# Six instead of three first-layer products per unit by the inner scheme, with the operations ordered by a table

## Chip, cores and metric

The kernel runs on one core of a Trainium2 chip. The metric is the device time of one launch in microseconds; less is better. All data are float32.

## The reference

```python
# q, k, v: (8 batches, 8 heads, 576 tokens, 64);  w_in (512, 2048);  w_out (2048, 512);  alpha (2048)
k_p = k.reshape(B, H, 72, 8, D).mean(axis=3)
v_p = v.reshape(B, H, 72, 8, D).mean(axis=3)
scores = np.matmul(q, k_p.transpose(0, 1, 3, 2)) / np.sqrt(D)
attn = np.exp(scores - scores.max(axis=-1, keepdims=True))
attn = attn / (attn.sum(axis=-1, keepdims=True) + 1e-09)
x = np.matmul(attn, v_p).transpose(0, 2, 1, 3).reshape(4608, 512)
h = x @ w_in
s = np.sin(alpha * h)
g = h + s * s / (alpha + 1e-09)
out = g @ w_out
```

So it is an attention over pooled keys and values, and behind it two matrix products with a sine nonlinearity between them.

## The kernel before, in words

**Stages.** There are eight batches of 576 tokens for the attention and nine units of 512 tokens for the first layer. While unit u runs through the first layer, the attention of batch u+1 is computed beside it, so that its values are there when unit u+1 starts. The results g of the first layer go to a buffer in DRAM (`g_bridge`). The second layer (`outputs`, line 1312 for its matmuls) then runs over the eight batches and reads g back.

**Products.** Both layers use a scheme of Strassen's kind: a product of 2 x 2 blocks is computed with seven products of blocks instead of eight. In the first layer a unit has four column groups J = 0 to 3, and each has seven products, numbered 1 to 7: 28 products in a unit. A plain product (`product`, line 834) is four matmuls of 128 x 128 weights with 256 columns. It adds into a PSUM bank; `begin` takes the four banks b1, b6, b5 and b7 of a group from five that rotate (0 to 4). Banks 5 to 7 serve the attention and the intermediate results of the inner scheme.

**Inner scheme.** `inner_product` (line 1014) computes a product once more by seven smaller ones, each one matmul with 128 columns. It comes in four pieces: `a` (two matmuls into bank 6 or 7, then two ACT copies, lines 1018 and 1020), `b` (two matmuls, one ACT copy, line 1024), `d` (one matmul, one DVE add, line 1029) and `e` (two matmuls). Each piece needs the copies of the one before, so other matmuls are written between the pieces. In units 1 to 6 it is used for product 5 of J = 2 and 3 and for product 1 of J = 3: three products of 28. The sums that it needs are made by GpSimd (POOL): those of the weights once, in unit 0 (`inner_w_in`), those of x in each unit (`inner_x`).

**Around a product.** ACT copies b1 to b6, b6 to b7 and b5 to the tile p5 (line 810), computes the sines (984) and squares (991). DVE adds p5 and the sines (809) and finishes a group (`finish`, 1036), then SP stores its g (`store_g`, 1050). The tile for g has two buffers, so group J+2 writes where group J was stored from.

**The attention's steps.** For one batch: `k_t` (keys transposed), `two_scores` (scores, in two blocks of 64 and 80 recorded matmuls, line 308), shifts (the row maximum is taken and subtracted, DVE, 331 and 332), `exp` on ACT (357), `norm` (row sums on DVE, product on POOL, 365), `turn` (DVE transposes, 491 to 501), `move` (16 transfers, 511), `all_values` (600 and 613, and ACT copies into x, 527). `turn_q` transposes a later batch's q on DVE (219, 224) and moves it with 16 transfers (234). `load_k`, `load_v` and `load_q` fetch, and POOL adds the rows that are pooled (131). `sums_of_x` forms the four sums of x that the products take (DVE, 804).

**Order.** The program is written out by hand: `hidden` runs over 28 slots of a unit, seven to a column group, and `carry` says which attention step goes into which slot. Each engine executes its instructions in the order in which the program issues them, and SP's queue holds back all transfers behind one that waits. In the kernel before, the two blocks of scores are in slots 3 and 5 (in front of products 2 and 3 - that is, behind products 6 and 7 - of J = 0), the exps in slots 8 to 10, the values in slot 25.

Of the kernel before, what the change touches and what calls it, by code (L numbers as in the profile page):

```python
# [24 lines left out]

class Kernel:
    def __init__(self, tc, q, k, v, w_in, w_out, alpha, out):
        self.tc, self.nc = tc, tc.nc
# [12 lines left out]
        self.T = self.S // 4  # L56

        self.gd = self.nc.dram_tensor("g_bridge", (2, self.NJ * JW, P, self.B * self.S), F32, kind="Internal").ap()

    def home(self, i, shape):  # L60

        return (self.xp if i < 2 else self.xq).tile(shape, F32, name=f"home{i}")
# [15 lines left out]
    def q_tile(self, i):  # L78

        return self.qp.tile([P, 5 * self.H * self.D], F32, name=f"q{int(i)}")  # L80
# [35 lines left out]
    def load_k(self, b, e):  # L116
# [3 lines left out]
        t = self.kvp.tile([P, 2048], F32, name="kvin")[:NP * m, 0:3 * POOL * D]  # L120
        self.nc.sync.dma_start(out=t, in_=self.k[b, NP * e:NP * e + NP].rearrange("h (p x) d -> (h p) (x d)", x=3 * POOL))
        if b not in self.kp:
            self.kp[b] = self.ap.tile([NP * m, 3, 2, D], F32, name="kp")
# [9 lines left out]
    def load_v(self, b):  # L133

        nc, D, H = self.nc, self.D, self.H
        vm, vz = self.vp[b] = self.ap.tile([P, H // 2, D], F32, name="vm", bufs=2), self.ap.tile([P, H // 2, D], F32, name="vz", bufs=2)
        t = self.kvp.tile([P, 2048], F32, name="kvin")[:].rearrange("p (h x) -> p h x", h=4)
        x = self.kvp.tile([P, POOL * D], F32, name="vr", bufs=1)[:]
# [40 lines left out]
    def load_v_rows(self, b, main, rest):  # L179
# [6 lines left out]
        self.vp[b] = self.ap.tile([P, self.H // 2, self.D], F32, name="vm", bufs=2), self.ap.tile([P, self.H // 2, self.D], F32, name="vz", bufs=2)  # L186
# [19 lines left out]
    def turn_q(self, b, part):  # L206
# [8 lines left out]
        if part == 0:  # L215
            for e in range(2):
# [3 lines left out]
                if e == 0:  # L220
                    self.finish_before()
# [17 lines left out]
    def new_tr(self):  # L239
        return self.ap.tile([P, 20 * 5 * 32], F32, name="tr")[:]  # L240
# [8 lines left out]
    def attention(self, b):  # L249
# [44 lines left out]
        def two_scores(j):  # L294

            x = (self.turn + 1) % 5
# [22 lines left out]
        def shifts(i, m, ps):  # L319
# [6 lines left out]
            for z, o in zip(ps, y):  # L326
                w = list(z.shape)[:-1]
                mx = self.sm.tile([P, 12], F32, name="mx2")[:, 0:m * (1 + i % 2)]
# [15 lines left out]
        def shift(i, e, ps):  # L344

            n = rows[i]
            mx = self.sm.tile([P, NP], F32, name="mx")
# [11 lines left out]
        def norm(i):  # L359

            n = E(i).shape[1]
            sm = self.sm.tile([P, 12], F32, name="sm2")[:, 0:n]
# [4 lines left out]
        def new_a():  # L367
            self.aM = self.ap.tile([P, 4, 736], F32, name="aM")
# [71 lines left out]
        def norm_rest():  # L440

            n = 64
            sm = self.sm.tile([P, H], F32, name="sm")
# [146 lines left out]
        def all_values():  # L590
# [16 lines left out]
            nc.scalar.copy(out=self.sm.tile([P, 1], F32, name="order")[:], in_=rest[:, 1, 0:1])  # L607
# [7 lines left out]
            self.behind_order()  # L615
            self.behind_order = lambda: None
# [152 lines left out]
    def inner_w_in(self):  # L769

        w = self.q_tile(0)[:]
        at = 0
        for p, J0 in ((5, 2), (1, 3)):
            n = self.NJ - J0
# [31 lines left out]
    def hidden(self, u, extra):  # L806
# [7 lines left out]
        def begin(J):  # L814
# [5 lines left out]
            if two and J > 1:  # L820
                G.i5 = self.inner_product(G, 5, b5, 7)
# [757 lines left out]
```

## Time and profile before

| quantity | value |
|---|---|
| timed runs | 906.38, 906.35, 905.76 us; median 906.35 us |
| profiled execution | span 902.6 us from its first to its last instruction; no time of its own is given beside it |
| what lies around the span | 906.35 - 902.6 = 3.75 us by the median |
| start of unit 1 (k transpose in front of it) | 84.44 us |
| units 1 to 6, period | 55.06 us |
| last product of the first layer ends | about 515 us |
| second layer, PE without a stop | 537.40 to 898.3 us |
| 16 DMA engines, busy share in a middle unit | 0.68 to 0.71 |
| granted TensorE clock | 1.000 |

The span is that of one profiled execution. PE is TensorE's matmuls, PEld its weight loads, DVE VectorE, ACT ScalarE, POOL GpSimd, SP the engine that issues most transfers. Each float32 matmul appears as two instructions. Records of matmuls overlap; the distance between their starts, not their length, is what one costs.

### The profile page before, as it was taken

Reading aid. Unit: us, or ns where it says so; the run is one execution under the profiler, and the core shown is the slowest. Engines: PE = TensorE matmul, PEld = TensorE weight load, DVE = VectorE, ACT = ScalarE, POOL = GpSimd, SP = SyncE. Lnnn points to the kernel's source line nnn. Section 1 sums busy time; section 2 is a strip of 40 time slices with the busy share of each in tenths; the row PEclk is TensorE's granted clock in tenths of the full one; section 3 lists DMA queues with packets and bytes.
Section 4 is the critical chain, followed back from the end, with each engine's and each line's share of the span. In section 5 each row is a group of like instructions: output and inputs, shape, how many; then the busy total and the mean of one; then the engine's idle time right before and its main releaser. Section 6 shows DMA issues by size and latency. Waiting matters only on the chain.

```text
span 902.6 us, 17941 instructions
## 1 busy us (share of the span) xinstructions
PE 895.0 (99%) x7014; PEld 815.8 (90%) x7014; DVE 677.4 (75%) x1011; ACT 448.3 (50%) x1070; POOL 210.5 (23%) x216
## 2 busy tenths in 40 slices
PE   8999999999999999999999999999999999999998
PEld 5787888888888888888888999999999999999997
DVE  7685766768577685764458799979798888889895
ACT  5696776877768778687976611111111111111111
POOL 4788552824438253430000000000000000000000
PEclk9999999999999999999999999999999999999999
DMA  9965867759586595648216346261618162534401
GB/s 261 245 200 158 220 163 202 196 167 251 139 213 186 177 230 143 176 146 293 93 72 227 102 141 199 59 194 38 224 27 230 33 197 67 172 92 127 137 15 40
DMA packets 128747, 141.13 MB, mean 156 GB/s; under 512 B 46920, under 2 KB 95704, under 8 KB 128664
## 3 DMA queue, kind: packets, MB, share of 16 engines
q1 hardware_dynamic: 125880, 137.88, 53.2%
q10 hardware_dynamic: 2784, 2.11, 0.9%
q8 instruction: 56, 0.92, 0.4%
q14 instruction: 27, 0.22, 0.1%
HBM read 75.37 MB, written 47.19 MB: 136 GB/s over the span
## 4 chain that ended last, share of the span: by engine, by line
PE 91%; DMA 3%; DVE 2%; POOL 2%; SPq 1%; issue 0%; ACT 0%; DVEq 0%; POOLq 0%
PE PS L834 42%; PE PS L1312 41%; PE PS L1014 3%; PE PS L308 2%; PE PS L600 2%; DMA a<-in_moe_w_in_dram 2%; DMA kvin<-in_v_dram 1%; SPq L669 1%; PE PS L613 1%; DVE x L1267 1%; DMA h<-in_k_dram 1%; POOL kvin L131 0%; POOL as L675 0%; DVE s L1267 0%; POOL ex L365 0%
## 5 line engine op out<-in xcount | busy, mean ns | idle before, releaser
L834 PE MATMUL PS<-home,a 128*128 128x256 f32 x1104 | 257.9, 381 | 0.7 <-ACT home L527 0.5
L834 PEld LDWEIGHTS PS<-home,a 128*128 128x128 f32 x1104 | 205.2, 190 | 34.1 <-issue 5.0
L834 PE MATMUL PS<-home,as 128*128 128x256 f32 x768 | 183.0, 382 | 0.0
L834 PEld LDWEIGHTS PS<-home,as 128*128 128x128 f32 x768 | 141.6, 190 | 19.8 <-ACT PS L810 1.2
L1312 PE MATMUL PS<-s,wb 128*128 128x144 f32 x896 | 119.1, 286 | 0.0
L1362 POOL TENSOR_TENSOR cc<-cc,cb 128x576 f32<-128x576 f32 x1 | 2.0, 1976 | 501.8 <-DVE cb L1267 501.8
L1312 PEld LDWEIGHTS PS<-s,wb 128*128 128x128 f32 x896 | 113.7, 190 | 0.1
L991 ACT ACTIVATE s<-s,c 128x256 f32<-128x256 f32 (+1 forms) x228 | 113.5, 564 | 0.0
L809 DVE TENSOR_TENSOR h<-PS,p 128x512 f32<-128x512 f32 x72 | 49.2, 683 | 64.2 <-PE PS L834 36.3
L131 POOL TENSOR_TENSOR kvin<-kvin 96x768 f32<-96x768 f32 (+3 forms) x42 | 71.6, 1705 | 69.5 <-DMA kvin<-in_v_dram 67.9
L1440 ACT COPY PS<-PS 128x144 f32<-128x144 f32 x56 | 14.7, 263 | 145.0 <-PE PS L1312 135.5
L984 ACT ACTIVATE s<-h,al 128x256 f32<-128x256 f32 x144 | 65.6, 510 | 39.4 <-DVE h L809 39.3
L1312 PE MATMUL PS<-r,wb 128*128 128x144 f32 x512 | 73.3, 286 | 0.3 <-DVE r L1267 0.3
L1312 PE MATMUL PS<-s,a 128*128 128x144 f32 x512 | 73.2, 286 | 0.0
L1036 DVE TENSOR_TENSOR h<-PS,s 128x512 f32<-128x512 f32 x36 | 24.7, 687 | 59.8 <-ACT s L991 59.8
L984 ACT ACTIVATE s<-PS,al 128x256 f32<-128x256 f32 x144 | 60.1, 470 | 18.6 <-PE PS L834 17.7
L1312 PEld LDWEIGHTS PS<-r,wb 128*128 128x128 f32 x512 | 67.1, 190 | 0.5 <-DVE r L1267 0.5
L1312 PEld LDWEIGHTS PS<-s,a 128*128 128x128 f32 x512 | 67.1, 190 | 0.0
L810 ACT COPY PS<-PS 128x512 f32<-128x512 f32 x72 | 41.5, 576 | 35.0 <-PE PS L834 30.4
L1460 ACT COPY PS<-PS 128x144 f32<-128x144 f32 x56 | 14.7, 263 | 88.1 <-PE PS L1312 88.1
L1312 PE MATMUL PS<-s,we 128*128 128x144 f32 x384 | 54.9, 286 | 0.0
L1312 PE MATMUL PS<-x,wb 128*128 128x144 f32 x384 | 54.9, 286 | 0.0
(215 smaller groups left out, 1407.7 us busy)
## 6 DMA issues: line engine op xcount, KB each, us to landing
g_bridge<-h SPq DMA_DIRECT2D x72, 512.0 KB
r<-g_bridge SPq DMA_DIRECT2D x31, 1152.0 KB
out_dram<-o SPq DMA_DIRECT2D x122, 72.0 KB
kvin<-in_k_dram SPq DMA_DIRECT2D x14, 576.0 KB
q<-in_q_dram SPq DMA_DIRECT2D x7, 1024.0 KB
kvin<-in_v_dram SPq DMA_DIRECT2D x14, 512.0 KB
aM<-tr SPq DMA_DIRECT2D x54, 92.0 KB
aM<-tr SPq DMA_DIRECT2D x54, 88.0 KB
```

The source lines that it names most:

```text
L131: self.nc.gpsimd.tensor_tensor(out=t[..., 0:w] if w > D else out, in0=t[..., 0:w], in1=t[..., w:2 * w], op=OP.add)
L308: nc.tensor.matmul(ps[e][r0 + r:r0 + r + q.shape[-1], h, :], q[s], kb[s, hp, :], start=True, stop=True)
L600: nc.tensor.matmul(o[r:r + 64], w, x, start=start and i < 2, stop=False, skip_group_check=True)
L809: add = lambda o, x, y: nc.vector.tensor_tensor(out=o, in0=x, in1=y, op=OP.add)
L810: copy = lambda o, x: nc.scalar.copy(out=o, in_=x)
L834: nc.tensor.matmul(ps[:, jj, :], self.A[p][:, kk, f * P:(f + 1) * P], x[:, kk, :], start=(start and n == 0), stop=(kk == 1), skip_group_ch ...
L984: self.nc.scalar.activation(out=G.s[:, i, jj, j, :], in_=src[:, jj], func=AF.Sin, scale=self.al[:, f:f + 1])
L991: self.nc.scalar.activation(out=x, in_=x, func=AF.Square, scale=self.c[:, f:f + 1])
L1014: nc.tensor.matmul(o, W[m][:, G.J - J0], X[m], start=start and n == 0, stop=True, skip_group_check=True)
L1036: add = lambda o, x, y: self.nc.vector.tensor_tensor(out=o, in0=x, in1=y, op=OP.add)
L1312: nc.tensor.matmul(out, W[:, J // 2, J % 2, :], A[:, J, :], start=(start and J == 0), stop=(J == self.NJ - 1), skip_group_check=True)
L1440: nc.scalar.copy(out=x1[:, 0, :], in_=x0[:, 1, :])
```

## The change

It has three parts.

1. *Inner scheme.* `self.J0 = 1`: products 5 and 1 of J = 1, 2 and 3 go by the inner scheme, six products of 28 in units 1 to 6. POOL makes six sets of weight sums of 128 columns each in place of one set of 256 and one of 128 columns. The sixth set lies in the tile `last`, so the sums of x move to `ex` and to a tile of their own.
2. *Order.* The engines' calls between `begin` and `flush` are recorded instead of issued. `flush` finds from the regions that each operation reads and writes which one must come before which, and issues them so that PE keeps program order, and ACT, DVE, POOL and SP the order of a table (`PLAN`, one number per operation; every middle unit has the same numbers, shifted by 5406). `hidden` becomes one straight sequence for a group.
3. *Places.* In units 1 to 6 product 5 of J = 0 (`late`) goes behind product 7 and behind piece `a` of the next group's product 1. The scores use its bank in place of the next free one, and go in front of product 6 and into the middle of product 2. The exps are recorded in slot 8, `k_t` in slot 27 instead of 26. In the second layer the loads of the next batch's g go to the end of steps 3, 4 and 5 instead of the beginning of steps 3 and 5.

```diff
+    def flush(self):
+        ...
+        self.edges()
+        lines = {e: [t for t in self.tasks if t.eng == e] for e in self.ENG.values()}
+        for e, x in lines.items():
+            for n, t in enumerate(x):
+                t.at = n if e == "PE" else t.unit * UNIT.get(t.key[0][0], 0) + self.plan.get(t.key, 0)
+            x.sort(key=lambda t: t.at)
+        left = {t: len(t.pre) for t in self.tasks}
+        for _ in self.tasks:
+            ready = [x for x in lines.values() if x and not left[x[0]]]
+            x = min(ready, key=lambda x: (x[0].eng != "PE", x[0].at))
+            t = x.pop(0)
+            t.f(*t.a, **t.k)
+            for u in t.suc:
+                left[u] -= 1
+UNIT = {"u": 5406, "p": 4790}
+PLAN = """
 ...
+u.sums_of_x : 3771 3759 7998 8420
+u.two_shifts : 3795 3804
+u.exp : 4551 4272 4571 4561
 ...
+"""
 two_scores:
-            x = (self.turn + 1) % 5
+            x = (self.turn + (1 if b < 2 else 4)) % 5
 inner_w_in:
+        at = [w[:, 4 * P * i:4 * P * (i + 1)] for i in range(5)] + [self.last[:, 0:4 * P]]
+        for J in range(self.J0, self.NJ):
+            for p in (5, 1):
+                ...
+                self.sums(((s1, L(1, 0), L(1, 1), OP.add), (s2, s1, L(0, 0), OP.subtract), (s3, L(0, 0), L(1, 0), OP.subtract), (s4, L(0, 1), s2, OP.subtract)))
 hidden, one group:
+            extras()
+            if not two:
+                product(G, 1, G.b1, start=True)
+            copy(G.b6[:], G.b1[:])
+            late = 0 < u < self.B - 1 and not two
+            extras()
+            if not two and not late:
+                product(G, 5, G.b5, start=True)
+            extras()
+            product(G, 6, G.b6, (0, 1))
+            if two:
+                G.i5.a()
+            product(G, 6, G.b6, (2, 3))
+            copy(G.b7[:], G.b6[:])
+            if two:
+                G.i5.b()
+            extras()
+            product(G, 2, G.b1, (0, 1))
+            if two:
+                G.i5.d()
+            if J == 0:
+                for f in extra["mid"]:
+                    f()
+            product(G, 2, G.b1, (2, 3))
+            if two:
+                G.i5.e()
+            ...
+            product(G, 7, G.b7, (0, 1))
+            if N and not late:
+                N.i1.a()
+            product(G, 7, G.b7, (2, 3))
+            if late:
+                N.i1.a()
+                product(G, 5, G.b5, start=True)
+                copy(G.p5[:], G.b5[:])
+            add(G.g[:, 1, :, 1], G.b7[:], G.p5[:])
+            ...
+            if N:
+                N.i1.b()
+            product(G, 3, G.b6, (0, 1))
+            if N:
+                N.i1.d()
+            product(G, 3, G.b6, (2, 3))
+            ...
+            if N:
+                N.i1.e()
+            product(G, 4, G.b7)
+            self.last_parts(G)
 carry:
-                at((3, 5)[i], A.two_scores, i)
-            at(6, A.two_shifts)
+            at(1, A.two_scores, 0)
+            at("mid", A.two_scores, 1)
+            at(4, A.two_shifts)
 outputs:
-                if n == 3 and u + 1 < self.B:
-                    self.load_g(u + 1, ("r11", "r12", "r22"))
-                if n == 5 and u + 1 < self.B:
-                    self.load_g(u + 1, ("r21",))
+            if st and u + 1 < self.B:
+                self.load_g(u + 1, {3: ("r11", "r22"), 4: ("r12",), 5: ("r21",)}.get(n, ()))
```

## The prediction, written before the changed kernel was run

> **What bounds the kernel now.** I read the page first: its busy rows and its chain of work that ended last.
>
> ```profile
> span 902.6 us, 17941 instructions
> ...
> PE 895.0 (99%) x7014; PEld 815.8 (90%) x7014; DVE 677.4 (75%) x1011; ACT 448.3 (50%) x1070; POOL 210.5 (23%) x216
> ...
> PE 91%; DMA 3%; DVE 2%; POOL 2%; SPq 1%; issue 0%; ACT 0%; DVEq 0%; POOLq 0%
> ```
>
> The chain is TensorE (PE) for 91%. Line 834 (first-layer products) and line 1312 (second layer) carry 42% and 41% of the span. So work taken off PE is worth its full length, if nothing else becomes late. The table of windows shows how much room the others have in one of the six middle units (their period, from one k transpose to the next, 137.80 to 192.86 us, is 55.06 us):
>
> ```profile
> 86.00:141.00 55.00, 55.00 (x446) 47.15 (x446) 39.21 (x64) 41.35 (x96) 25.52 (x25) 1.00 0.68 179
> ```
>
> After the interval and its length the columns are PE, PEld, DVE, ACT, POOL, granted clock, DMA share, GB/s. ACT has 14 us of idle time in 55, DVE 16; the clock is full. PE's timeline gives the price of both kinds of product:
>
> ```profile
> 103.44 3.62 PE L834 MATMUL PS<-home,as 128*128 128x256 f32 x16
> 106.90 3.66 PE L834 MATMUL PS<-home,a 128*128 128x256 f32 x16
> ...
> 121.08 0.38 PE L1014 MATMUL PS<-home,q 128*128 128x128 f32 x2
> 121.30 0.39 PE L1014 MATMUL PS<-last,as 128*128 128x128 f32 x2
> 121.52 1.03 PE L834 MATMUL PS<-home,a 128*128 128x256 f32 x4
> 122.39 0.38 PE L1014 MATMUL PS<-home,a 128*128 128x128 f32 x2
> ```
>
> Records overlap, so starts count and not lengths. 16 instructions of 256 columns take 106.90-103.44 = 3.46 us, 0.216 each. Four of 128 columns take 121.52-121.08 = 0.44 us, 0.110 each. The four of 256 columns behind them take 0.87 us, with no gap: the inner scheme's pieces pass without a stop where 0.87 us of other products lies between them.
>
> **The change, part by part.**
>
> *Products.* Each matmul is two instructions here (a plain product writes 4 matmuls, 8 instructions are recorded). A plain product is 8 x 0.216 = 1.73 us, an inner one 7 matmuls, 14 x 0.110 = 1.54 us. Units 1 to 6 go from 3 inner products to 6: 18 products, 0.19 us each, **-3.4 us**, all on the bounding engine.
>
> *Cuts.* An inner product goes in as four groups. Of the 12 groups in a unit now, two or three have a next block of four that takes 0.91 instead of 0.87 us. Twelve more groups cost 0 to 12 x 0.05 = 0.6 us a unit; by the share that is slow now 0.1, less where the pieces sit between halves of one product. I take 0.08, **+0.5 us** in all (0 to 3.6).
>
> *Bank of the scores.* Now the first score matmul of a unit goes into the free bank, last read by the finishing add (line 1036) of the group before. The table of waits shows weight loads idle for it, 2.3 us in 6 times, and PE's starts show 0.14 us lost before the scores (146.71 to 146.85). The new bank is that of the postponed product 5, read last by an add two products earlier. Up to 0.8 us can go; part of the gap stays with every change of matmul shape (0.10 us behind the scores, where nothing is waited for). I take **-0.6 us**.
>
> *ACT and DVE work added.* An inner product adds copies of 0.375, 0.276 and 0.250 us on ACT (lines 1018, 1020, 1024) and one add of 0.43 us on DVE (1029). Three more a unit: ACT 41.4 to 44.1 us, DVE 39.2 to 40.5 us of 55. Cover: idle time. But a piece must be copied within the 0.87 us in which PE does other work: 0.22 us from PE to ACT, 0.375 us copy, 0.1 us back, leaves about 0.2 us. One sine in front (0.47 to 0.51 us) uses that up. The third group of columns now lives with the same windows for two products at once and loses nothing, so I take 0.05 a unit, **+0.3 us**; bounds 0 and 0.3 a unit (0 and 1.8).
>
> *Scores earlier and closer together.* Both score blocks move into column group 0: before product 6 and in the middle of product 2. Then, with nothing moved away, the first inner piece of group 1 writes bank 6, which the last scores fill and DVE must have emptied. From the first score matmul PE needs 1.26+1.73+0.87+1.46+0.87+1.73 = 7.92 us plus four changes of shape of 0.1, 8.3 us, before that piece. In that time DVE, by the table's order, does the first four shifts, two x sums, one reduction of 288 and one reduction and subtraction of 864 elements. From today's rows:
>
> ```profile
> 92.85 0.44 DVE L331 TENSOR_REDUCE mx<-PS 128x4 f32<-128x288 f32 x1
> ...
> 95.34 0.76 DVE L332 TENSOR_TENSOR ex<-PS,mx 128x576 f32<-128x576 f32 x1
> ...
> 101.40 1.05 DVE L331 TENSOR_REDUCE mx<-PS 128x12 f32<-128x864 f32 x1
> 102.48 1.06 DVE L332 TENSOR_TENSOR ex<-PS,mx 128x864 f32<-128x864 f32 x1
> ```
>
> DVE starts 1.06 us after the first scores (91.79), needs 92.85 to 96.10 = 3.25, two sums of 0.60 (line 804, median 0.69 with the overlap taken off), 0.48, and 101.40 to 103.54 = 2.14: 8.13 us. So at the median the chain ends 0.17 us early: cost **0**. Line 804 reaches 1.08 us while POOL computes, and POOL will be doing the x sums for the inner scheme just then; two slow sums make it 8.9, and PE waits up to 0.6 us a unit (3.6 us). This is the thinnest cover of the change.
>
> [...]
>
> *exps, turns, moves, stores (the table).* The order on PE is program order; ACT, DVE, POOL and SP follow the table. Exps go in front of most of group 0's sines and leave two table loads of 1.28 us a unit, as now. SP carries 8 stores, 16 moves (0.59 us each, median), 16 transfers of turned q and 12 loads a unit. The table puts one half of group 1's store behind the first four transfers of turned q, which wait for their transposes. Group 3 writes the same buffer: its second add must wait until that store has landed, and the next unit's first scores wait for that add's bank. A load of similar size (v, issued 95.2, used 103.6, 1 MB) takes up to 8 us behind other traffic; a lone one of 0.5 MB I estimate at 4 us from its half. At 4 us it just fits: 0. Each us beyond costs 1 us a unit.
>
> *POOL, once.* The inner weights become 24 operations of 0.45 us in place of four of 0.72 and four of 0.46: 10.8 against 4.7 us, at the border of units 0 and 1. Today they end at 83.9, and the first inner piece would start at about 96.5 us; three fourth sums go behind unit 1's norms. Taken as 0; bounds 0 and 3 us once.
>
> *Start, second layer, tail.* The second layer runs 360.9 us without a stop; loads of g now go out one step's end later, with a step of 6.87 us each in hand. The start could win or lose about 1 us (waits before PE sum to 2.9 us, nearly all before 20 us). Taken as 0.
>
> **Sum.** -3.4+0.5-0.6+0.3 = -3.2 us on a profiled span of 902.6 us. The timed runs' median is 906.35, 3.75 us more, which lie outside the first and last instruction; the page gives no other time for this execution. The change doesn't touch them, so **906.35-3.2 = 903.1 us**. A measurement here can tell some 0.2%, 1.8 us, from no change.
>
> **Rivals.**
>
> *Slower: DVE's shifts hold the first inner piece (0.19).* Place: bank 6 at the end of group 0 in six units. Price: 0.6 us there, and then ACT, 80% busy, gets its copies late, so that some of the ten later pieces wait 0.05 to 0.1 each: together about 1 us, 6 us in all, 906.35-3.2+6 = 909.2. It decides from (3.2+1.8)/6 = 0.83 us a unit. For it: the margin is 0.17 us. Against it: PE's changes of shape, and the score reductions read PSUM, whose rows don't vary.
>
> *Slower: the late store (0.05).* Landing 6 us after issue costs 2 us a unit, 12 us: about 915.
>
> *Slower: weight loads set the pace (0.03).* 14 loads instead of 8 a product; at their 190 ns each that is 6 x 0.19 x 18 = 20.5 us, 926.9. Against it: four loads pass in 0.44 us today. [...]
>
> *Within 0.2% (0.13).* Saving eaten by cuts and waits of 0.25 to 0.8 us a unit: about 905.5. That includes the case that the new pieces simply wait out what they save.
>
> *Faster still (0.16).* The table also closes waits in unit 0 and at PE's start, and cuts cost nothing: -3.4-0.8-2 = 900.2.
>
> *Forecast (0.44).* 901.3 to 904.5, likeliest 903.1.
>
> **How the numbers follow.** Faster 0.44+0.16 = 0.60; same 0.13; slower 0.19+0.05+0.03 = 0.27. The forecast's own range is 901.3 to 904.5. The range reaches from the better case to the first rival: 900.0 to 909.3; it leaves out the late store, the weight loads and thin ends.
>
> **What would show it.** Right: 252 instructions of line 1014's kind become 504, with about 0.110 us between starts; the period of a middle unit is 54.4 to 54.6 us instead of 55.06; no entry above 0.2 us a unit under PE or its loads for DVE. Wrong: waits of PE on the shifts' subtraction or on line 1029's adds, a DVE add waiting for a store to g_bridge, a period above 55.1 us, or a start (to the end of unit 0, 84.4 us) that moved by more than 1 us.

## The result: slower by 1.0%, and the profile after

The changed kernel takes 915.31 us (median of four runs, 913.51 to 916.89); the kernel before took 906.37 us on the same chip. The ratio is 1.0102, 95% interval 1.0085 to 1.0120. I had forecast 903.1 us, with 900.0 to 909.3 as the range. The profiled execution took 915.4 us of its own, with a span of 913.4 us. The page and two rows of the table of windows:

```profile
span 913.4 us, 18293 instructions
...
PE 898.0 (98%) x7122; PEld 818.5 (90%) x7122; DVE 667.4 (73%) x1029; ACT 457.9 (50%) x1112; POOL 196.6 (22%) x232
...
PE 91%; DMA 3%; DVE 2%; SPq 2%; issue 0%; ACT 0%; DVEq 0%
```

```profile
30.00:45.00 15.00, 11.05 (x108) 8.99 (x102) 6.97 (x17) 7.65 (x13) 5.98 (x6) 0.77 1.01 235
152.00:207.00 55.00, 54.57 (x463) 47.03 (x462) 38.47 (x67) 42.40 (x102) 22.33 (x25) 1.00 0.68 193
```

PE still carries the chain, but it isn't full any more. From 30 to 45 us it is busy for 11.05 of 15 us, at a granted clock of 0.77 (0.77 is the last column but two). The kernel before was busy for 15.00 of these 15 us, at 1.00. PE's timeline there:

```profile
29.50 0.72 PE L156 MATMUL PS<-h,q 64*64 64x72 f32 x16
34.17 3.78 PE L156 MATMUL PS<-home,as 128*128 128x256 f32 x8 [3.95 <-ACT PS L156]
37.74 3.19 PE L156 MATMUL PS<-home,a 128*128 128x256 f32 x8
40.77 1.04 PE L156 MATMUL PS<-ident,q 128*128 128x128 f32 x8
```

All recorded operations carry line 156, so the tiles say what is what. Product 6 of unit 0 waits 3.95 us for ACT. Then products 6 and 2 take 3.57 and 3.03 us from start to start, in place of 1.83 and 1.73: half clock (from 35 to 40 us the granted clock is 0.50). In the kernel before, product 6 started at 29.23 and the q transposes at 32.79; now they start at 34.17 and 40.77. That makes 4.94 us up to the start of product 6, 3.95 of them this wait, and 3.04 us for the clock. ACT's timeline, first the changed kernel, then the one before, shows why:

```profile
25.80 0.58 ACT L156 COPY aM<-PS 64x512 f32<-64x512 f32 x1 [0.29 <-PE PS L156]
32.91 0.62 ACT L156 COPY q<-q 128x512 f32<-128x512 f32 x1 [6.54 <-DMA a<-in_moe_w_in_dram]
33.54 0.57 ACT L156 COPY PS<-PS 128x512 f32<-128x512 f32 x1
```

```profile
22.01 0.57 ACT L810 COPY PS<-PS 128x512 f32<-128x512 f32 x1 [1.26 <-PE PS L834]
...
30.18 2.69 ACT L97 COPY q<-q 128x512 f32<-128x512 f32 x5
```

The copy `PS<-PS` takes b1 to b6 for product 6. Before, it ran at 22.01, as soon as product 1 was there. The table gives it the key 2004 and gives 2003 to a copy of batch 1's q. That one has to wait for a transfer until 32.91 us, and holds everything behind it. (The profile puts the wait down to a load of w_in; that the order of the loads decides it is shown by e2 below.) The transfer is late too: the table puts parts of v and w_in ahead of it in SP's queue, so that q's two loads go out at 18.26 and 21.80 us in place of 15.37 and 16.11.

Unit 0 ends at 92.79 us in place of 84.44: **+8.35**. Units 1 to 6 cost 2.9 us more, where I had expected 3.2 us less. The middle units 2 to 5 take 55.59 us on average in place of 55.11. One wait comes back in each of them; here it is in unit 4 (all engines' timeline):

```profile
283.28 0.38 PE L156 MATMUL PS<-home,q 128*128 128x128 f32 x2
283.50 0.39 PE L156 MATMUL PS<-ex,as 128*128 128x128 f32 x2
283.73 1.25 PE L156 MATMUL PS<-home,a 128*128 128x256 f32 x6
...
284.42 1.63 POOL L156 TENSOR_TENSOR ex<-ex,sm 128x864 f32<-128x864 f32 x1 [1.80 <-ACT s L156]
...
285.15 1.98 DVE L156 TENSOR_TENSOR h<-h,s 128x1024 f32<-128x1024 f32 x1
...
287.43 1.03 PE L156 MATMUL PS<-home,as 128*128 128x256 f32 x4
...
288.44 0.39 DVE L156 TENSOR_TENSOR PS<-PS,m 128x256 f32<-128x256 f32 x1
...
288.89 0.49 PE L156 MATMUL PS<-home,q 128*128 128x128 f32 x2 [0.43 <-DVE PS L156]
```

The first three rows show the inner pieces at their price: 0.22 us for two, 0.110 each, and no gap behind them. Then piece `e` of product 1 for J = 2 (288.89) waits for DVE's add `PS<-PS,m`. It starts 1.46 us after the group ahead of it instead of 0.87: 0.59 us lost. DVE is late because the last add of J = 0 (`h<-h,s`) takes 1.98 us beside POOL's normalisation; in a pause of POOL's (e5 below) an add of this shape takes 1.22.

One correction to the sum's base: in a later run the kernel before took 904.39 us with the same span of 902.6 us, 1.8 around it and not 3.75. By this its profiled execution was 1.9 us better than its median. So the traces differ by 10.8 us, the times by 8.9.

### The profile page after: what moved, and what is told of

It is laid out like the page before. It is cut to its first block, busy times and chain, and to the rows that moved or that the text cites. A ratio compares the mean times of both kernels' runs of the same rounds, so it can differ in the third digit from the quotient of the medians.

```text
span 913.4 us, 18293 instructions
## 1 busy us (share of the span) xinstructions
PE 898.0 (98%) x7122; PEld 818.5 (90%) x7122; DVE 667.4 (73%) x1029; ACT 457.9 (50%) x1112; POOL 196.6 (22%) x232
## 4 chain that ended last, share of the span: by engine, by line
PE 91%; DMA 3%; DVE 2%; SPq 2%; issue 0%; ACT 0%; DVEq 0%
PE PS L156 91%; SPq L156 2%; DMA a<-in_moe_w_in_dram 2%; DMA home<-in_k_dram 1%; DMA kvin<-in_v_dram 1%; DVE h L156 1%; DVE tr L156 0%; DMA q<-tr 0%; DVE ex L156 0%; DVE PS L156 0%; DVE mx L156 0%; DVE sm L156 0%; ACT L156 0%; ACT q L156 0%; DVE c L156 0%
## 5 line engine op out<-in xcount | busy, mean ns | idle before, releaser
L156 ACT COPY PS<-PS 128x144 f32<-128x144 f32 (+4 forms) x312 | 114.4, 369 | 296.6 <-PE PS L156 282.2
L156 PE MATMUL PS<-home,a 128*128 128x256 f32 (+1 forms) x1080 | 253.2, 376 | 1.4 <-DVE h L156 0.5
L156 PEld LDWEIGHTS PS<-home,a 128*128 128x128 f32 x1080 | 196.8, 191 | 30.1 <-issue 4.6
L156 PE MATMUL PS<-home,as 128*128 128x256 f32 (+1 forms) x792 | 188.6, 374 | 4.0 <-ACT PS L156 4.0
L156 ACT ACTIVATE s<-s,c 128x256 f32<-128x256 f32 (+1 forms) x216 | 116.7, 577 | 4.5 <-DVE c L156 2.1
L156 ACT ACTIVATE s<-PS,al 128x256 f32<-128x256 f32 x144 | 64.5, 471 | 33.5 <-PE PS L156 33.3
L156 DVE TENSOR_TENSOR h<-PS,s 128x512 f32<-128x512 f32 x72 | 49.0, 681 | 36.3 <-ACT s L156 35.9
L156 POOL TENSOR_TENSOR kvin<-kvin 96x768 f32<-96x768 f32 (+3 forms) x42 | 66.0, 1573 | 5.5 <-DMA kvin<-in_v_dram 4.8
L156 DVE TENSOR_TENSOR h<-h,s 128x1024 f32<-128x1024 f32 x36 | 50.2, 1394 | 18.9 <-ACT s L156 18.9
L156 POOL TENSOR_TENSOR ex<-ex,sm 128x576 f32<-128x576 f32 (+1 forms) x28 | 35.3, 1272 | 86.3 <-DVE sm L156 75.0
```

The source lines that it names most:

```text
L156: t.f(*t.a, **t.k)
```

## Experiments

Every kernel below moves or leaves out something of the changed kernel; the first column of ratios is against the kernel before on the same chip. "End" is the k transpose that closes unit 0, "unit 1" runs from there to the next, "middle" is the mean of units 2 to 5. (In the kernel before, `k_t` stood one product earlier from unit 1 on, so its unit 1 reads 53.36; like for like it is 55.1.) "Clock" is the time lost to half clock in the profiled run, from rows of 5 us of the table of windows. These four columns are of one profiled run, the median is of all.

| kernel | median us | ratio (95%) | end | unit 1 | middle | clock |
|---|---|---|---|---|---|---|
| before | | | 84.44 | 53.36 | 55.11 | 0 |
| changed | 915.31 | 1.0102 (1.0085-1.0120) | 92.79 | 55.83 | 55.59 | 3.45 |
| e1_pairs_late | 917.83 | 1.0141 (1.0124-1.0158) | 93.24 | 56.36 | 55.55 | 1.7 |
| e2_loads_early | 912.65 | 1.0079 (1.0057-1.0101) | 92.34 | 56.35 | 55.53 | 3.45 |
| e3_both | 912.18 | 1.0073 (1.0049-1.0097) | 86.84 | 58.81 | 55.20 | 0 |
| e4_fill | 916.51 | 1.0120 (1.0105-1.0135) | 91.64 | 57.49 | 55.79 | 3.45 |
| e5_no_train | 910.59 | 1.0053 (1.0038-1.0067) | 84.37 | 57.15 | 55.32 | 0 |
| e6_turns_first | 915.73 | 1.0112 (1.0082-1.0142) | 84.48 | 64.55 | 55.25 | 3.4 |
| e7_add_late | 916.64 | 1.0113 (1.0081-1.0145) | 86.22 | 65.02 | 55.55 | 3.45 |
| e9_pool_order | 913.69 | 1.0095 (1.0073-1.0118) | 84.47 | 61.52 | 55.41 | 0 |
| e10_add_later | 917.24 | 1.0140 (1.0113-1.0168) | 84.83 | 60.27 | 56.68 | 1.7 |
| e11_add_alone | 909.90 | 1.0056 (1.0041-1.0071) | 84.46 | 59.76 | 55.40 | 1.7 |
| e12_fill_free_bank | 914.15 | 1.0099 (1.0080-1.0117) | 90.52 | 57.35 | 55.69 | 0 |
| e13_row_behind_loads | 909.83 | 1.0048 (1.0034-1.0063) | 84.40 | 58.21 | 55.14 | 0 |
| e14_add_on_gpsimd | 906.64 | 1.0017 (1.0001-1.0033) | 86.32 | 57.07 | 54.84 | 1.7 |
| r1_no_squares | 912.51 | 1.0075 (1.0051-1.0099) | 86.61 | 59.20 | 55.40 | 1.7 |
| r2_no_pool_rows | 909.39 | 1.0043 (1.0026-1.0060) | 84.98 | 58.88 | 55.32 | 0 |
| r3_no_last_add | 905.49 | 1.0006 (0.9989-1.0022) | 84.77 | 58.91 | 54.55 | 1.7 |
| r4_all_relieved | 907.19 | 1.0024 (1.0010-1.0038) | 88.60 | 58.40 | 54.78 | 1.7 |

Theory at the outset: the start is lost in ACT's queue, and 8 us come back when the queue is put right. Rivals: the load itself holds the start; the middle units are what costs; the slow matmuls have another cause than the wait.

**The start: e1 to e4.** Two edits of the table, apart and together, and one of PE's program.

```diff
 e1:
-0.pairs_q : 2299 2612 2003 2005 2755
+0.pairs_q : 2297 2298 2299 2300 2301
 e2 (e3 has both):
-0.load_v : 5536 5537 1606 4600 660 507 3399 3602 3718
+0.load_v : 5536 5537 4600 4600 4600 4600 3399 3602 3718
-0.load_w_in_part : 1725 2031 2255 1019 5540 683 1828 1956
+0.load_w_in_part : 1725 2031 2255 1721 5540 1720 1828 1956
 e4, ahead of product 6 of unit 0, J = 0 (matmuls of no use into bank b7):
+nc.named("fill ", lambda: [nc.tensor.matmul(G.b7[:], ...) for _ in range(4)])()
```

> The changed kernel with one line of its table altered: in unit 0 ScalarE's five copies of batch 1's q into pairs take the keys 2297 to 2301 (all five behind the copies into x), in place of 2299, 2612, 2003, 2005 and 2755, so that none of them stands ahead of the copy of product 1 for which product 6 waits. Theory (the loss of the start is this place in ScalarE's queue): product 6 of unit 0 starts at about 29.5 us in place of 34.17 and runs at full clock; but TensorE then comes to the transposes of q at about 33.3, while the load of q still lands at about 32.9 and five copies of 0.62 follow, so some 3 us of waiting moves there; the time falls by 4 to 8, to 907.5-911. Rival (the load of q is what holds the start, wherever its copies stand): the wait moves whole to the transposes, 915 +- 1. Rival (the start is not what costs; units 1 to 6 are): under 1 us gained.

> The changed kernel with SyncE's queue at the start in the order of the kernel before: three of the four small loads of v's last rows, and two quarters of w_in, go behind the two loads of batch 1's q instead of ahead of them. ScalarE's order stays, with two copies of q ahead of the copy that product 6 waits for. Theory (place in ScalarE's queue): q lands 2 to 3 us sooner, at about 30, so product 6 starts at about 31.5 in place of 34.17; the idle time of TensorE falls from 3.95 to about 1.5 us and with it the clock stays up: 908.5 to 911. Rival (the clock falls by something else than the idle time): 912.5 (2.7 gained, 3 of half clock kept). Rival (loads are bound by the memory, order is nothing): 915 +- 1.

> The changed kernel with both edits: q's copies behind the copy that product 6 waits for, and q's loads ahead in SyncE's queue as in the kernel before. Theory: unit 0 as in the kernel before, its last transposes of k at about 84.5 to 85.5 in place of 92.79, the time 915.3 - 8 = 907.3 (906.5 to 908.5); what is left above the kernel before (906.4) is the 2.9 us that units 1 to 6 lost less what the second layer gained and the time around the span. Rival (most of the loss is elsewhere): 911 or more.

> The changed kernel with four matmuls of 128x512 in f32 (about 0.87 us each at full clock, of no use, into a bank that is overwritten next) put ahead of product 6 in unit 0, so that TensorE works through most of the 3.95 us in which it waits for ScalarE's copy. The wait itself stays. Theory (the idle time lets the clock fall, and products 6 and 2 then run at half speed): product 6 still starts at about 34.2, but runs at 0.216 us an instruction and not at 0.446; the window 30 to 45 us has a granted clock of 1.00 in place of 0.77; 3.0 us gained, 912.3. Rival (the matmuls behind the wait are slow for another reason, operands or ports): nothing gained or up to 0.5 lost, 915.3 to 915.8.

Measured: product 6 starts at 31.13 (e1), 30.88 (e2) and 29.57 us (e3). In e1 and e3 no half clock follows it: e3 lost nothing in the whole run, and the 1.7 us of e1 lie between 60 and 70 us. So the two causes of the first wait are right. But the time doesn't follow: e1 is 2.5 us slower than the changed kernel, and e2 and e3 gain 2.7 and 3.1 us where 4 to 9 were expected. The trace of e1 shows where the gain went (all engines' timeline):

```profile
54.05 1.26 POOL L156 TENSOR_TENSOR as<-a,as 128x512 f32<-128x512 f32 x1
54.36 7.20 DVE L156 TENSOR_TENSOR h<-h,s 128x1024 f32<-128x1024 f32 x1
...
55.27 2.35 POOL L156 TENSOR_TENSOR kvin<-kvin 128x1024 f32<-128x1024 f32 x1
...
57.58 1.26 POOL L156 TENSOR_TENSOR a<-a,a 128x512 f32<-128x512 f32 x1
58.80 0.45 POOL L156 TENSOR_TENSOR q<-a 128x128 f32<-128x128 f32 x1
59.22 1.26 POOL L156 TENSOR_TENSOR kvin<-kvin 128x512 f32<-128x512 f32 x1
61.48 0.68 DVE L156 TENSOR_TENSOR h<-PS,p 128x512 f32<-128x512 f32 x1
...
62.21 1.22 PE L156 MATMUL PS<-home,a 128*128 128x256 f32 x2 [4.83 <-DVE h L156]
```

DVE's add of two SBUF tiles takes 7.20 us. Five POOL instructions follow one another without a gap until 60.48, and the add ends 1.08 us later, at 61.56: about the 1.22 us that it takes in e5 in POOL's pause. PE waits 4.83 us for the add behind it, and its clock falls again, to 0.83 on average from 60 to 70 us. In the changed kernel PE came 5 us later, and this add met only the end of the row (2.89 us). So the first stall had hidden a second one. e4 tells nothing of the clock: its own matmuls waited 4.74 us for ACT's reads of the bank that they wrote, and they ran in bf16, 0.415 us each in place of the 0.87 that I had expected.

**The second stall: e5.** In unit 0 the add goes behind DVE's last shift.

```diff
 0.: entry 49 (last add of J = 0)
-4777
+4786
```

> e3_both with one more key: in unit 0 VectorE's last addition of J=0 (h<-h,s, 128x1024, both operands in SBUF) goes from in front of the addition that the sines of J=1 wait for to behind the last shift, 4777 to 4786. In e3_both this addition took 4.13 us (7.20 in e1_pairs_late, 6.23 in e2_loads_early, 1.2 at its shortest), and ended each time when GpSimd's row of instructions without a gap had ended; TensorE then waited 1.76 (4.83, 3.86) for the addition queued behind it. Theory (VectorE's addition with two operands in SBUF can't run until GpSimd pauses, and what is queued behind it waits): in the new place it takes under 2 us, the wait of 1.76 is gone, unit 0 ends at about 85.0 in place of 86.8, and the runs lie closer together, since no wait nears the 4 us behind which the clock fell: 910 to 911.5 (part is eaten by the wait for the transposes of q at the start of unit 1). Rival (it is the data that came late, or ScalarE's squares): it takes 4 us in the new place too, and TensorE waits as before: 912.2 +- 1.

```profile
54.06 1.27 POOL L156 TENSOR_TENSOR kvin<-kvin 128x512 f32<-128x512 f32 x1
...
55.75 1.22 DVE L156 TENSOR_TENSOR h<-h,s 128x1024 f32<-128x1024 f32 x1
...
57.22 1.15 POOL L156 TENSOR_TENSOR ex<-ex,sm 128x576 f32<-128x576 f32 x1 [1.89 <-DVE sm L156]
```

The same add takes 1.22 us in POOL's pause, and unit 0 ends at 84.37 us, as in the kernel before (84.44). In this run the whole +8.35 of unit 0 is gone. The profiled run came to 907.08 us with a granted clock of 0.999; the other nine have 0.996 to 0.998, which in the profiled runs of the table goes with 3.45 or 1.7 us of half clock, and lie between 909.58 and 912.82.

The new place is no safe one. All later kernels but e8 and e12 keep it. In e5 the add starts 0.42 us behind the end of POOL's row. In nine of the eleven later profiled runs it takes 1.22 to 1.63 us, but 2.66 in e7 and 3.04 in r1, where the row came some 2 us later against it (r1's timeline of all engines):

```profile
56.31 3.04 DVE L157 TENSOR_TENSOR h<-h,s 128x1024 f32<-128x1024 f32 x1
...
57.00 1.26 POOL L157 TENSOR_TENSOR kvin<-kvin 128x512 f32<-128x512 f32 x1
...
60.16 3.69 PE L157 MATMUL PS<-home,as 128*128 128x256 f32 x16 [1.02 <-DVE sm L157]
```

Unit 0 then ends at 86.22 (e7) and 86.61 us (r1).

**Unit 1: e6, e9, e13.** What is left in e5's unit 1 is a wait of the scores (PE's timeline of e5):

```profile
88.19 0.73 PE L156 MATMUL PS<-kblk,q 64*64 64x72 f32 x32
90.20 0.31 PE L156 MATMUL PS<-kblk,q 64*64 64x72 f32 x2 [1.27 <-DMA q<-tr]
90.75 0.72 PE L156 MATMUL PS<-kblk,q 64*64 64x72 f32 x30 [0.24 <-DMA q<-tr]
```

The change moved the scores from 91.8 us (kernel before) to 88.2; the sixteen transfers of turned q that they read are issued until about 92.

```diff
 e6:
-0.turn_q : 4873 4870 7364 5756 5758 5755 5759 5761 ... 5768
+0.turn_q : 4873 4870 7364 5752 5752 5752 ... 5752        (and a store of h: 5556 to 5752)
 e9 = e6 with the pooled rows behind the inner sums on POOL:
-u.load_v 3070 3080 3081; u.pool_v 3061 3064 3067 3069; u.pool_k 3087 3088 3091
+all ten 3094
 e13 = e5 with the row of transfers behind the loads of v:
+0.turn_q : 4873 4870 7364 5761 5761 ... 5761            (and the store: 5556 to 5752)
```

> e5_no_train with SyncE's queue at the end of unit 0 put in order: the sixteen transfers of q's transposes (q<-tr) go out in one row, ahead of the loads of v and the stores of h that stood between them, and a store of h goes behind the row of aM<-tr. In e3_both the last q<-tr was issued at about 96 us (90.9 in the kernel before) and the scores of unit 1 waited 1.2 + 0.5 for it. Theory: the waits of the scores for q<-tr in unit 1 go (from about 2.3 us in all to under 0.5), and 2 to 3 us come off: 907.5 to 909. Rival (the transfers take their time whatever their order): same as e5_no_train.

> e6_turns_first with GpSimd's order in the middle units changed: its sums for the inner scheme (x<-home, ex<-home) go ahead of its sums of the rows of v and k (keys 3061 to 3091 to 3094). In e6_turns_first GpSimd stood idle 13.96 us with the first sum of v's rows at its head, since that edit had put the load of v behind the transposes of q; the sums for the inner scheme were queued behind it, TensorE waited 4.67 for them and its clock fell behind the wait (3.4 us). Theory (a queue in order, its head waiting for a transfer): both go, 8 us, and unit 1 takes 1 to 2 us less than in e5_no_train, where the scores waited 1.27 and 0.55 for q<-tr: 906.5 to 908.5. Rival (GpSimd is simply full at the start of unit 1): the sums for the inner scheme are late all the same, 911 or more.

> e5_no_train with SyncE's sixteen transfers q<-tr of unit 0 in one row as in e6_turns_first, but behind the loads of v for unit 1 (keys 5761, the loads have 5753 to 5760), so that GpSimd gets the rows of v as early as in e5_no_train; a store of h stands behind the aM<-tr row. In e5_no_train the last q<-tr was issued at about 92 us and the scores of unit 1, which the change moved to 88.2 us (91.8 in the kernel before), waited 1.3 and 0.5 for them. Theory: the last q<-tr goes out at about 91, 0.5 to 1.5 us come off and GpSimd isn't late: 909 to 910. Rival (GpSimd's queue is held again, as in e6_turns_first): 913 or more.

e6 and e9 missed. In e6 the loads of v now went out behind the row, POOL's first sum of v's rows waited for them, and the sums for the inner scheme were queued behind it (POOL's timeline, then PE's):

```profile
94.01 0.73 POOL L156 TENSOR_TENSOR vr<-vr 128x256 f32<-128x256 f32 x1 [13.96 <-issue]
...
99.50 2.82 POOL L156 TENSOR_TENSOR kvin<-kvin 128x1024 f32<-128x1024 f32 x1 [1.85 <-DMA kvin<-in_v_dram]
102.28 0.45 POOL L156 TENSOR_TENSOR x<-home 128x128 f32<-128x128 f32 x1
```

```profile
102.78 0.80 PE L156 MATMUL PS<-x,q 128*128 128x128 f32 x2 [4.67 <-POOL x L156]
```

e9 took this wait away, but only 3 us of unit 1 with it: DVE then waited 2.78 us for a store of h that e6's row had also pushed back, and PE 2.12 us for DVE, the late store of my rivals, made by my own edit. e13 brings 909.83 against 910.59, within the scatter: its row still ends at 91.8 us, and PE waits 1.23 us in the second block. SP's order alone doesn't mend unit 1. That the scores stand too early there for these transfers is what the rows say; no run put the scores back.

**The middle units: e7, e10, e11.** The add of J = 0 goes behind the add of the inner scheme; e7 on top of e6, e10 on top of e9, e11 on e5 alone.

```diff
 u.: entry 60 (last add of J = 0 in units 1 to 6)
-5260
+5283   (e7)        +5285   (e10, e11)
```

> e6_turns_first with one key of the middle units: VectorE's last addition of J=0 (h<-h,s, 1.99 us beside GpSimd's normalisation) goes behind the addition of the inner scheme of product 1 for J=2 (5260 to 5283), for which TensorE waited 0.43 in each of the six units (0.59 from start to start). Theory: this wait is gone, the middle units take 54.5 us in place of 55.15 and 6 x 0.59 = 3.5 us come off: 904 to 905.5, below the kernel before. Rival (VectorE has no room there, the wait only comes back at the next addition or at the sines): under 1 us.

> e9_pool_order with one key of the middle units: VectorE's last addition of J=0 (h<-h,s) from 5260 to 5285, behind both the addition of the inner scheme of product 1 for J=2 (5282) and the addition that frees the bank into which ScalarE copies next (5284); e7_add_late had put it between the two, and the wait of 0.43 at the first came back as 0.37 at the copy. Theory: neither wait is left, a middle unit takes 54.5 us in place of 55.1, 6 x 0.5 = 3 us less than e9_pool_order: 903.5 to 905.5, below the kernel before. Rival (the time of a middle unit is set by VectorE, each wait removed comes back at the next): within 1 us of e9_pool_order.

> e5_no_train with the same key alone (5260 to 5285), without the edits of SyncE's and GpSimd's queues. Theory: the middle units from 55.1-55.6 to 54.5-55, unit 1 still waits 1.8 for q<-tr: 906.5 to 908.5 against 910.6. Rival as for e10_add_later: within 1 us of 910.6.

The rival wins. e7 (916.64 against e6's 915.73) gains nothing. In e11 the 0.59 us at piece `e` are gone, and 0.55 us come back some 5 us later, where piece `b` of product 5 of J = 2 now waits for ACT's copy (timeline of all engines):

```profile
286.80 0.65 DVE L156 TENSOR_TENSOR h<-PS,p 128x512 f32<-128x512 f32 x1
...
287.54 0.36 ACT L156 COPY PS<-PS 128x256 f32<-128x256 f32 x1 [0.74 <-DVE h L156]
...
287.95 0.49 PE L156 MATMUL PS<-ex,q 128*128 128x128 f32 x2 [0.29 <-ACT PS L156]
```

That copy in turn waits 0.74 us for DVE, which had the moved add at 283.69 and its transposes to do first. The middle units stay at 55.40 us (55.32 in e5). In e10, with POOL's rows moved as well, that wait for ACT is 1.3 us in each of them. Moving the add on the same engine doesn't free the engine.

**What holds the middle units: r1 to r4.** One engine after another is relieved of work, in e5.

```diff
 in flush, ahead of edges():
+r1: leave out units 1-6 ACT: all Square
+r2: leave out units 2-7 POOL: u.load_v, u.pool_v, u.pool_k
+r3: leave out units 1-6 DVE: h<-h,s of all four J
+r4: all three
```

> e5_no_train with ScalarE relieved: in units 1 to 6 its squares (s<-s,c, about 3.1 us for each of the four groups, 12 us a unit) are left out of the program, everything else stays in its place. The product count, and so TensorE's own work, is the same: 22 x 1.73 + 84 x 0.110 + 2.63 for the scores + 3.66 for values and k = 53.6 us a unit, against 55.05 to 55.64 measured in e5_no_train, so that 1.5 to 2 us a unit are waits. Theory (the waits come from ScalarE's queue): a middle unit falls to 54.0-54.5, 910.6 - 6 x 1 = 904.5 (903 to 906.5). Rival (they come from VectorE behind GpSimd): under 0.3 us a unit, 909 to 911. Rival (TensorE's own floor is 55, my sum is too low): no change.

> e5_no_train with GpSimd relieved: from unit 2 on its sums of the rows of v and k are left out (some 10 us a unit; vm, vz and kp keep old data), the sums for the inner scheme and the normalisation stay. Theory (VectorE's instructions with two operands in SBUF wait for GpSimd and delay the shifts of the scores): the second block of scores is no longer late (1.46 from its start to the next product in place of 1.7 to 2.1), 0.3 to 0.6 us a unit for five units, 907.5 to 909. The wait of 0.43 behind the addition of J=0, which runs beside the normalisation, stays. Rival (ScalarE): within 0.7 us of 910.6.

> e5_no_train with VectorE relieved: in units 1 to 6 the last addition of each group (h<-h,s 128x1024, 1.2 to 2.0 us, four a unit) is left out. Theory (VectorE's queue holds TensorE at the addition of the inner scheme for J=2, 0.59 from start to start): the wait is gone and, other than when the addition is only moved (e11_add_alone, where 0.45 + 0.10 came back at the next copy), nothing comes in its place: 0.5 to 0.6 us a unit, 907 to 907.8. Rival (the next wait, ScalarE's copy behind the squares, stands just behind it and takes its place): under 0.2 us a unit, 909.5 to 911.

> e5_no_train with all three left out (ScalarE's squares and VectorE's last additions in units 1 to 6, GpSimd's sums of rows from unit 2 on). Theory (the change's saving in TensorE's work, 0.57 us a unit, is there but is taken back by waits for the three other engines): a middle unit comes to 53.7-54.2 us, as TensorE's own work says, 910.6 - 6 x 1.3 = 903 (901.5 to 904.5). Rival (TensorE itself takes 55 us for this order of products): above 908.

Without some 11 us of ACT's work (42.4 to 31.5 in a window of 55 us), and without 13.5 of POOL's (22.5 to 8.9), a middle unit is as long as before (55.40, 55.32). Without DVE's last adds, all four of a unit, it takes 54.71, 54.48, 54.41 and 54.60 us, 54.55 on average: the prediction said 54.4 to 54.6. So the saving of the inner products is there, and DVE's add of two SBUF tiles is what takes it back. r4 adds nothing to r3 (54.78). Its unit 0 ended at 88.60 in the profiled run because PE's work between 6 and 17 us took nearly twice its time (32 score matmuls 1.24 in place of 0.73 us), 4.0 us in all; the rows of the table of windows give a clock of 1.00 there all the same, and the cause is open. My 53.7 to 54.2 for r4's middle units was too low.

**With the whole computation: e14.** The add of J = 0 goes to POOL, behind the normalisation, on top of e13.

```diff
+eng = self.nc.gpsimd if Q.J == 0 and 0 < Q.u < self.B - 1 else self.nc.vector
+eng.tensor_tensor(out=Q.g[:, :, :, 1], in0=Q.g[:, :, :, 1], in1=Q.s[:, :, :, 1], op=OP.add)
 u.: entry 60
-5260
+3098
```

> e13_row_behind_loads with the last addition of J=0 in units 1 to 6 (h<-h,s 128x1024) taken from VectorE and given to GpSimd, behind its normalisation of 864 elements (key 3098), where GpSimd stood idle; the whole computation is there. r3_no_last_add, which left the last addition of all four groups out, had middle units of 54.41 to 54.71 us in place of 55.05 to 55.64. Theory (the time that VectorE spends on this addition, doubled beside GpSimd, holds TensorE in the middle units): 54.5 to 54.9 us a unit, 2.5 to 3.5 us less than e13_row_behind_loads: 906 to 907.5. Rival (on GpSimd, 2.35 us long, it holds VectorE's transposes or its own normalisation behind it, and the wait comes back): within 1 us of e13_row_behind_loads.

The same stretch of a unit in e14 (timeline of all engines):

```profile
277.98 1.63 POOL L156 TENSOR_TENSOR ex<-ex,sm 128x864 f32<-128x864 f32 x1 [1.81 <-DVE sm L156]
...
279.57 2.37 POOL L156 TENSOR_TENSOR h<-h,s 128x1024 f32<-128x1024 f32 x1
...
280.99 1.03 PE L156 MATMUL PS<-home,as 128*128 128x256 f32 x4
281.25 0.43 DVE L156 TENSOR_TENSOR PS<-PS,m 128x256 f32<-128x256 f32 x1
...
281.86 0.39 PE L156 MATMUL PS<-home,q 128*128 128x128 f32 x2
```

The piece starts 0.87 us after the group ahead of it, with no wait. Three of the four middle units take 54.36, 54.73 and 54.37 us; one takes 55.89. 906.64 us is 3.2 us below e13 and some 8 below the changed kernel, but not below the kernel before (1.0017, 1.0001 to 1.0033): in the profiled run unit 1 still costs 2 us more, and unit 0 ended 1.9 us late, 1.7 of it by a fall of the clock between 5 and 15 us (0.90 in the first five, 0.76 in the second). What comes behind wins 1.8 of these 3.9 us back: the span is 904.7 us against 902.6.

**The clock alone: e12.** Ten matmuls of no use into a bank that is free then.

```diff
+x = self.psum([P, 4, P], 6)
+nc.named("fill ", lambda: [nc.tensor.matmul(x, ...) for _ in range(10)])()
 product(G, 6, G.b6, (0, 1))
```

> The changed kernel with ten matmuls of no use (128x512 in bf16, 0.415 us each by e4_fill) ahead of product 6 of unit 0, now into a bank that nobody uses then (those of e4_fill waited 4.74 us themselves, for ScalarE's reads of the bank that they wrote, so the idle time stayed). ScalarE's copy comes as late as in the changed kernel. Theory (the clock falls because TensorE stands idle for about 4 us): product 6 starts at 34.2 as before, but products 6 and 2 take 1.8 us each, the granted clock is 1.00 throughout, 3.4 us gained: 911.9. Rival (the clock falls by the load of the whole chip or by the time since the start): 915.3, half clock as before.

```profile
30.31 2.33 PE L156 MATMUL PS<-full 128*128 128x512 bf16 x10
34.47 1.99 PE L156 MATMUL PS<-home,as 128*128 128x256 f32 x8 [1.82 <-ACT PS L156]
36.30 1.89 PE L156 MATMUL PS<-home,a 128*128 128x256 f32 x8
38.02 1.04 PE L156 MATMUL PS<-ident,q 128*128 128x128 f32 x8
```

The ten took 0.21 us each (the 0.415 of e4 is about twice that, which I take for half clock), so 1.82 us of idle time stayed, and products 6 and 2 ran at 1.83 and 1.72 us. Product 6 starts as late as in the changed kernel, but with 1.82 us of idle time in place of 3.95 the granted clock from 30 to 45 us is 1.00 in place of 0.77: here it was the idle time that cost the clock. Of the 2.75 us won up to the q transposes (38.02 against 40.77), 2.27 are left at the end of unit 0 and 0.75 at the end of unit 1 (57.35 in place of 55.83): 914.15 us, a ratio of 1.0099 against 1.0102.

**Without the table: e8.** Every engine in the order of recording.

```diff
-t.at = n if e == "PE" else t.unit * UNIT.get(t.key[0][0], 0) + self.plan.get(t.key, 0)
+t.at = n
```

> The changed kernel with its table left out: every engine's instructions stand in the order in which they are recorded. The products and the inner scheme are the same. Theory (the table is what loses the time in the start, by places that fit no measured time, but it does carry the middle units): the start has its own stalls, the middle units are slower than 55.4 us by 1 to 5 us each, since the last sines, squares and additions of a group then stand ahead of the next group's copies: 920 to 950. Rival (the table is worse than none): below 912.

1125.18 us (two runs; ratio 1.2425, 1.2338 to 1.2512). The new program depends on its table for more than 200 us; my estimate of 5 to 35 was far off.

## Why the prediction was wrong, point by point

- **Products, -3.4: right.** 0.110 us a piece, and 54.41 to 54.71 us a unit (r3) where DVE is out of the way; e14 shows it with everything computed.
- **Weight loads: rightly dismissed:** the inner pieces keep their 0.110 us from start to start (283.28 to 283.50 us above). **Second layer and POOL once: right.** The second layer takes 0.5 us less, and PE waits for no inner weights.
- **Start "taken as 0, could win or lose about 1 us": this step failed, and it is most of the miss.** It measured +8.35. I had read the table for the middle units and not for unit 0. There it held three things, the first two of which can be seen in the table and the trace of before together: a copy that waits for a load ahead of one that PE waits for (e1); loads in front of that load (e2); and, hidden behind these, a DVE add beside a row of POOL's (e5). e3 takes all but 2.4 us of it away from unit 0, and e5 all, in its profiled run.
- **"Cover: idle time" in ACT and DVE work: failed in the middle units.** I checked ACT's copies within their 0.87 us and gave DVE's add of piece `d` nothing, because DVE was idle for 16 us in 55. The add stands behind the last add of J = 0 and POOL's normalisation. It cost 0.59 us a unit, more than the net 0.53 that the whole sum was to save. An engine's idle share said nothing about this place; the order in front of one instruction did.
- **Shifts' chain, 0 with 0 to 0.6 a unit: right, PE has no wait at the first inner piece.** The second block of scores did take 1.65 to 2.13 us to the next product in four of six units, against 1.46 before, some 0.24 us a unit. But where the profile of a later run names what it waited for there, it is the transfers of turned q (0.15 us in e5, 0.42 in e7, 0.48 in e14), and r2, without the pooled rows, won no more than 1.2 us. The rival built on this chain (909.2) had the right engine and the right partner, VectorE beside GpSimd, but the wrong place; that its 6 us are about what the middle units lost against the forecast (+0.48 in place of -0.53 a unit) is luck. The start alone carried the time beyond it.
- **Scores earlier: a term was missing.** I followed the shifts behind the scores and not the transfers ahead of them. In unit 1 these end at 92 us, the scores start at 88. As soon as unit 0 is on time, unit 1 takes 2.0 us (e5), 3.1 (e13) and 3.8 us (r2) more than the 55.1 of before, and all three lost nothing to half clock; these waits are the first part of it.
- **Late store: not in the changed kernel**, only in e9.
- **The base:** 1.9 us, as told above.

In some runs one middle unit takes an extra microsecond. In e14 (55.89) it is the scores, which wait 0.21 and 0.48 us for turned q, 1.1 us from start to start. In the changed kernel (56.57) the second block of scores takes 2.13 in place of 1.65 us, and the matmuls of the values lose another 0.8 us; the profile names no cause for these. Open: that cause, and whether the scores' old slot would mend unit 1.

## What to carry to other kernels

When an order becomes a table, read it against the trace at the places where its times are least certain, the start above all: for each instruction that the bounding engine waits for, list what stands ahead of it on its engine and which transfer that waits for. A stall that is removed only shows the next, which had been hiding behind it; follow one marker per stage (here the end of unit 0, unit 1, the middle units) instead of the total. A place that fits by 0.4 us in one profiled run need not fit in the next. And idle time of an engine is no cover for a new instruction unless it lies in front of that instruction.

## What the runs showed of the hardware

- **DVE's add of two SBUF tiles waited for POOL, in e1 for a whole row of its instructions.** In the kernel before, the add `h<-h,s` (line 1036) takes 1.17 to 2.26 us, its form with a PSUM input, of half the size, 0.63 to 0.69. In the changed kernel, e1 and e3 the slow adds end 1.08 to 1.09 us after POOL's last instruction: in e1 61.56 after 60.48 (7.20 us in all), in e3 56.68 after 55.59 (4.13), in a middle unit of the changed kernel 287.13 after 286.05 (1.98). They had started 0.90 (middle unit) to 6.12 us (e1) before that instruction ended. In the middle unit one POOL instruction was in the way; in e1 it was five that follow without a gap. But a row isn't always waited out. In the kernel before (timeline of all engines):

```profile
146.51 0.46 POOL L794 TENSOR_TENSOR ex<-home 128x128 f32<-128x128 f32 x1
146.71 1.33 DVE L1036 TENSOR_TENSOR h<-h,s 128x1024 f32<-128x1024 f32 x1
...
146.92 1.44 POOL L794 TENSOR_TENSOR ex<-home,ex 128x128 f32<-128x128 f32 x1
```

Here the add waits only for the instruction that is running, ends 1.07 us after it (148.04 after 146.97), and POOL's next one takes 1.44 us, where the same operation took 0.45 at 146.09. What decides between the two these runs don't show.
- **Waits of 3.86 to 4.83 us also cost clock.** After idle times of 3.95, 4.83, 3.86, 4.74 and 4.67 us (changed kernel, e1, e2, e4, e6) the clock fell (in the changed kernel to 0.50 from 35 to 40 us); what was lost is 1.7 or 3.4 to 3.45 us, nothing between. After 1.76 (e3) and 1.82 us (e12) nothing was lost. But 1.7 us were also lost behind a wait of 2.91 us in e10, and behind waits of 1.61 and 0.53 us in e11 and 2.02 and 0.27 in r3, while r2 lost nothing behind 1.56 and 0.48: the length of the wait alone doesn't decide. What does, and why the loss comes in two sizes, these runs don't show.
